# First pairs of a retention and gated feed-forward kernel: the last query multiply behind a mask, its transposes into another bank, and two groups of matmuls issued earlier

## The chip, the cores and the metric

The program runs on one core of a Trainium2 chip. The core has TensorE (PE in the profile; PEld is its weight load), VectorE (DVE), ScalarE (ACT), GpSimd (POOL) and SyncE (SP), which issues the DMAs here. Each engine works through its own queue in order; engines wait for each other by semaphores. The metric is the device time of one execution in microseconds (us).

## The reference

The inputs q, k, v are 8 batches x 8 heads x 576 positions x 64 numbers, all float32. A retention layer feeds a gated feed-forward layer:

```
scores = q @ k^T / sqrt(64)
ret    = (scores * gamma[h] ** (i - j) for j <= i, else 0) @ v      # gamma[h] = 1 - 2 ** (-5 - h)
x      = ret, heads side by side                                    # 4608 x 512
out    = (sigmoid(x @ w_gate) * (x @ w_val)) @ w_out                # d_ff = 1536, out 4608 x 512
```

## The kernel before

**The mathematics.** The decay splits into a factor of the row and one of the column, so q is multiplied by a table (`qtab`, with 1/sqrt(64) in it) and k by another (`ktab`), and the scores need only a triangular mask. Positions are cut into chunks. Within a chunk, the masked scores are multiplied with v (`intra`); what comes from earlier chunks is a 64x64 state per head, the sum of k^T v so far, multiplied with q (`inter`). Both go into the same accumulator, and their sum is a block of `xT`, the transposed input of the feed-forward part.

**The beginning.** The first rows are handled in pairs of chunks: `PAIRS` names pair 0 and pair 1 (256 rows each, both of batch 0) and pair 2 (batch 1, much later). In a pair, chunk `a` lies on partitions `64a` to `64a+63`, with two rows `r` in each partition; the four head pairs `m` are treated in two halves `g`. For one pair and half:

- `cast_pair("k" or "q" or "v", A, g, ...)` turns a loaded tile into bfloat16; for k (GpSimd, L272) and q (VectorE, L272) it is the multiply with the table, for v a cast (GpSimd, L269).
- `turn("k" or "q", A, g, bank)` makes four transposes on TensorE (L312, into `kTp` or `qTp`) and one copy on ScalarE (L322).
- `pair_qk(A, g, banks)` makes 16 score matmuls (L331, `qkp`) into two banks and two masks on VectorE (L336, `ptp`).
- `first_st(A, a)` adds chunk a's k^T v to the running state in the accumulator `st_0` (8 matmuls, L362, `st`); `tile_sv(A, a)` copies the state out by two ScalarE copies (L371, `sbd`). The next `first_st` has to wait for that copy, since it adds to the same accumulator.
- `pair_intra(A, g, a)` is 8 matmuls (L429, `pvp`), `pair_inter(A, a)` 4 (L439, they read `sbd`), `pair_out(A, a, ...)` the copy into `xT` (L448).

`fill(n)` issues n matmuls of zeros, 512 columns each, into a bank that nobody reads (`idle`, L183); `idle_bank()` takes such a bank out of the pool.

**Banks.** The accumulators come from pools. `TR` is one bank (the k transposes, then chunk 1's `pvp`), `PV` is one (the q transposes, then chunk 0's `pvp`), `QK` two, `FF` (the pool `ffn_psum`) three, handed out in turn: the fourth request gets the first bank, when its last reader is done. `turn("q", 1, 1)` without a bank takes from `FF`.

**The order is written by hand** (`manual_schedule`): each engine gets its instructions in the order of the calls. After the pairs, the feed-forward of the first 512 columns begins, in halves of 256 columns (`h_half`: four matmuls each, L895; `gate` on ScalarE, L901; the product on VectorE, L898) for the first two of twelve feature blocks, then in full width (`h_both`, L816). From then on feed-forward matmuls (L712, L779) and the attention of the remaining chunks alternate.

**Loads.** All loads are issued by SP in the order k, q of the first two pairs, v, then the weights `wg`, `wv` for the first features, the second features and so on. Weights are cast to bfloat16 by GpSimd mostly (`cast_w`, L246); the first `h_half("v", ...)` needs both casts of `wv_sb` for features 0 and 1.

Of the kernel before, what the change touches and what calls it, by code (L numbers as in the profile page):

```python
# [16 lines left out]
def kernel(  # L17
# [88 lines left out]
    def half(x):  # L106
        return slice(x * 64, x * 64 + 64)
# [66 lines left out]
    def idle_bank():  # L174
        idle.append(ffn_psum.tile([P, 4, P], FP32, tag="ffn", name=f"idle_{len(idle)}"))
# [3 lines left out]
    def fill(n, parts=1):  # L179

        for i in range(n * parts):
            k = 4 // parts
            nc.tensor.matmul(idle[-1][:, 0:k, :], lhsT=blank, rhs=blank.unsqueeze(1).to_broadcast([P, k, P]),  # L183
                             start=True, stop=True)
# [74 lines left out]
    def cast_pair(nm, A, g, eng):  # L259

        if (nm, A) not in natural:
            natural[nm, A] = osb_pool.tile([P, 2, H, D], BF16, tag="osb", name=f"{nm}p_{A}")
        if nm != "v" and A == 2:
            o = natural[nm, A].rearrange("p r (m y) d -> p y m r d", y=2)[:, g]
        else:
            o = natural[nm, A][:, :, g * M:(g + 1) * M, :].rearrange("p r h d -> p h r d")
        i = parts.pop((nm, "pair", A, g))
        if nm == "v":
            eng(out=o, in_=i)  # L269
        else:  # L270
            tab = (ktab2 if nm == "k" else qtab2)[:, PAIRS[A][1], g * M:(g + 1) * M, :].unsqueeze(3).to_broadcast([P, M, 2, D])
            eng.tensor_tensor(out=o, in0=i, in1=tab, op=ALU.mult)  # L272
# [34 lines left out]
    def pair_t(nm, A, g, psum, tag, eng):  # L307
        ps = psum.tile([P, 2, 2, P], BF16, tag=tag, name=f"{nm}Tp_{A}_{g}")
        for i in range(2):
            for r in range(2):  # L310
                m = 2 * g + i
                nc.tensor.matmul(ps[:, i, r, :], lhsT=natural[nm, A][:, r, 2 * m:2 * m + 2, :], rhs=ident,  # L312
                                 is_transpose=True, start=(i == 0 and r == 0), stop=(i == 1 and r == 1))
        if nm == "k":
            if g == 0:
                turned["kp", A] = osb_pool.tile([P, M, 2, P], BF16, tag="osb", name=f"kT_{A}")
            o = turned["kp", A][:, 2 * g:2 * g + 2]
        else:
            if g == 0:
                turned["qp", A] = osb_pool.tile([P, M, 2 * P], BF16, tag="osb", name=f"qT_{A}")  # L320
            o = turned["qp", A][:, 2 * g:2 * g + 2, :].rearrange("p m (t r) -> p m r t", r=2)
        eng(out=o, in_=ps)  # L322

    def pair_qk(A, g, banks):
        ps = [psum.tile([P, 2, 2, P], FP32, tag=tag, name=f"qkp_{A}_{g}_{hh}") for hh, (psum, tag) in enumerate(banks)]
        for i in range(2):
            m = 2 * g + i
            for r in range(2):
                for a in range(2):
                    for hh in range(2):  # L330
                        nc.tensor.matmul(ps[hh][half(a), i, r, :], lhsT=turned["kp", A][half(hh), m, r, half(a)],  # L331
                                         rhs=turned["qp", A][half(hh), m, a * P:(a + 1) * P], start=True, stop=True)
        if g == 0:
            probs["p", A] = [att_pool.tile([P, M, 2, P], BF16, tag="T", name=f"ptp_{A}_{hh}", bufs=6) for hh in range(2)]
        for hh in range(2):
            nc.vector.tensor_tensor(out=probs["p", A][hh][:, 2 * g:2 * g + 2], in0=ps[hh],  # L336
                                    in1=trip.unsqueeze(1).to_broadcast([P, 2, 2, P]), op=ALU.mult)
# [18 lines left out]
    def first_st(A, a):  # L356

        if 0 not in st_tiles:
            st_tiles[0] = st_psum.tile([P, M, P], FP32, tag="st", name="st_0")
        for r in range(2):  # L360
            for m in range(M):
                nc.tensor.matmul(st_tiles[0][:, m, :], lhsT=natural["k", A][half(a), r, 2 * m:2 * m + 2, :],  # L362
                                 rhs=natural["v", A][half(a), r, 2 * m:2 * m + 2, :],
                                 start=(A == 0 and a == 0 and r == 0 and m == 0),
                                 stop=(A == 1 and a == 1 and r == 1 and m == M - 1), skip_group_check=True)

    def tile_sv(A, a, engs):
        b, a2 = PAIRS[A]
        sb = sbd[2 * A + a]
        for hh in range(2):  # L370
            engs[hh](out=sb[half(hh), :, half(hh)], in_=st_tiles[b][half(hh), :, half(hh)])  # L371
        state[b, 2 * a2 + a, 1] = sb
# [3 lines left out]
    def pair_tile(A, a, banks):  # L376

        s = 2 * A + a
        ps = [psum.tile([P, M // len(banks), P], FP32, tag=tag, name=f"pvp_{s}_{i}") for i, (psum, tag) in enumerate(banks)]
        pair_ps[s] = [(ps[m * len(banks) // M], m % (M // len(banks)), M // len(banks)) for m in range(M)]  # L380
# [39 lines left out]
    def pair_intra(A, g, a):  # L420
        s = 2 * A + a
        if s not in pair_ps:
            pair_tile(A, a, [(tr_psum, "tr") if a else (pv_psum, "pv")])
        for i in range(2):
            m = 2 * g + i
            ps, at_m, of = pair_ps[s][m]
            for r in range(2):
                for hh in range(2):
                    nc.tensor.matmul(ps[half(hh), at_m, :], lhsT=natural["v", A][half(a), r, 2 * m + hh, :],  # L429
                                     rhs=probs["p", A][hh][half(a), m, r, :],  # L430
                                     start=(at_m == 0 and r == 0), stop=(at_m == of - 1 and r == 1),
                                     skip_group_check=True)

    def pair_inter(A, a):
        b, a2 = PAIRS[A]
        c = 2 * a2 + a
        for m in range(M):
            ps, at_m, of = pair_ps[2 * A + a][m]
            nc.tensor.matmul(ps[:, at_m, :], lhsT=state[b, c - 1, 1][:, m, :],  # L439
                             rhs=turned["qp", A][:, m, a * P:(a + 1) * P],  # L440
                             start=False, stop=(at_m == of - 1), skip_group_check=True)

    def pair_out(A, a, *engs):
        t0 = (2 * A + a) * P
        k = M // len(engs)
        for i, eng in enumerate(engs):
            ps, at_m, _ = pair_ps[2 * A + a][i * k]
            eng(out=xT[:, i * k:(i + 1) * k, t0:t0 + P], in_=ps[:, at_m:at_m + k])  # L448
# [356 lines left out]
    def turn(nm, A, g, pool=ffn_psum, tag="ffn"):  # L805
        pair_t(nm, A, g, pool, tag, on_act)
# [34 lines left out]
    FF = [(ffn_psum, "ffn"), (ffn_psum, "ffn")]  # L841
    TR, PV = (tr_psum, "tr"), (pv_psum, "pv")
# [8 lines left out]
    turn("q", 0, 1, *PV)  # L851
    fill(3)
    cast_pair("q", 1, 0, nc.vector)
    cast_pair("q", 1, 1, nc.vector)
    pair_qk(0, 1, FF)
    turn("k", 1, 0, *TR)
    turn("q", 1, 0, *PV)
    fill(2)
    turn("k", 1, 1, *TR)
    turn("q", 1, 1)  # L860
    idle_bank()
    fill(1)
    pair_qk(1, 0, QK)
    fill(1)
    first_st(0, 0)
    tile_sv(0, 0, (on_act, on_act))
    pair_intra(0, 0, 0)
    pair_intra(0, 0, 1)
    pair_intra(0, 1, 0)
    pair_qk(1, 1, FF)  # L870
    pair_out(0, 0, on_act)
    pair_intra(0, 1, 1)
    first_st(0, 1)
    pair_inter(0, 1)
    tile_sv(0, 1, (on_act, on_act))
    pair_out(0, 1, on_dve)
    for a in range(2):
# [13 lines left out]
    def h_half(what, fc, x, ps):  # L891

        cols = slice(x * 256, x * 256 + 256)
        for kc in range(NKC):
            nc.tensor.matmul(ps, lhsT=(wg_sb if what == "g" else wv_sb)[:, kc, fc * P:(fc + 1) * P], rhs=xT[:, kc, cols],  # L895
                             start=(kc == 0), stop=(kc == NKC - 1))
        if what == "v":
            nc.vector.tensor_tensor(out=gvs[fc][:, cols], in0=gs[fc][:, cols], in1=ps, op=ALU.mult)  # L898

    def gate(fc, x, ps):  # L900
        nc.scalar.activation(out=gs[fc][:, x * 256:x * 256 + 256], in_=ps, func=AF.Sigmoid)  # L901

    def h_bank(psum, tag, name, n):
        return psum.tile([P, n, 256], FP32, tag=tag, name=name)
# [6 lines left out]
    pair_inter(1, 1)  # L911
    pair_out(1, 1, on_dve, on_act)
    gate(1, 0, g1)
    v0 = h_bank(ffn_psum, "ffn", "hv_0", 2)
    h_half("v", 0, 0, v0[:, 0])
    h_half("g", 0, 1, (g2 := h_bank(qk_psum, "qk", "hg_2", 2))[:, 0])
# [1 line left out]
    h_half("v", 1, 0, v0[:, 1])  # L918
    gate(0, 1, g2[:, 0])
    gate(1, 1, g2[:, 1])  # L920
    first_st(1, 1)
    tile_sv(1, 1, (on_act, on_act))
    for fc in range(2):
        h_half("v", fc, 1, h_bank(ffn_psum, "ffn", f"hv_{1 + fc}", 1)[:, 0])
# [162 lines left out]
```

## Time and profile before

| what | value |
|---|---|
| median of 4 runs | 329.68 us (329.45 to 330.28) |
| the profiled execution | 330.28 us, of which the span of the instructions is 328.6 us |
| PE busy | 318.1 us, 97% of the span |
| DVE, ACT, POOL busy | 149.1, 140.0, 104.8 us |
| chain that ended last | PE 91%, SP issue 3%, DMA 2%, DVE 1%, issue 1% |
| granted TensorE clock | 1.00 in every stretch of the stage table |
| DMA | q1: 54.44 MB, 68.9% of 16 engines' span; close to 100% of them busy until about 140 us |

Times in the profile count from the start of the span. A row of the timeline gives start, duration, engine, line, operation, the tiles (written `<-` read), how many instructions are merged, and in brackets how long the engine had been idle and what ended the wait. Matmuls overlap: a matmul's result comes about 0.16 us after the next one may begin, so the pace is read from one start to the next, not from durations. A row of the chain is start, duration and what the chain passed through.

The stretch that the change touches is the first 23 us. Up to about 12 us, the engines follow the loads as they land; from 22.8 us on, TensorE runs almost without a gap to the end.

### The profile page before, as it was taken

How to read it: one execution, taken by the hardware profiler on the slowest of the kernel's cores; microseconds unless marked ns; L12 is line 12 of the kernel's file. 1: busy time of each engine (PE TensorE's matmuls, PEld its weight loads, DVE VectorE, ACT ScalarE, POOL GpSimd, SP SyncE). 2: the span in 40 equal slices, each digit the busy share in tenths (PEclk: the TensorE clock that was granted, in tenths of full speed). 3: DMA queues.
4: the chain of work that ended last, by engine and by line, in shares of the span. 5: the costliest groups of instructions: out<-in, count | busy, mean ns of one | idle time of the engine just before them, and what ended most of it. 6: DMA issues, size and time to landing. Idle time of an engine off the chain costs nothing.

```text
span 328.6 us, 8723 instructions
## 1 busy us (share of the span) xinstructions
PE 318.1 (97%) x3586; PEld 170.5 (52%) x3620; DVE 149.1 (45%) x334; ACT 140.0 (43%) x315; POOL 104.8 (32%) x138
## 2 busy tenths in 40 slices
PE   7899999999999999999999999999999999999995
PEld 6564456856646654455444544454445544544443
DVE  5854747756615463345344543334444434404410
ACT  5645454554424444325533453335334533343321
POOL 5765647454534554008300840065003000000000
PEclk9999999999999999999999999999999999999999
DMA  7999999999997999908890799259804810010003
GB/s 215 309 358 381 340 295 230 220 188 201 185 208 156 220 231 217 170 0 190 203 229 22 141 205 254 47 112 224 212 0 101 324 61 0 34 69 31 3 32 96
DMA packets 144793, 55.14 MB, mean 168 GB/s; under 512 B 125168, under 2 KB 136688, under 8 KB 144752
## 3 DMA queue, kind: packets, MB, share of 16 engines
q1 hardware_dynamic: 144608, 54.44, 68.9%
q8 instruction: 28, 0.46, 0.6%
q10 hardware_dynamic: 144, 0.13, 0.1%
q14 instruction: 13, 0.11, 0.1%
HBM read 37.75 MB, written 9.44 MB: 144 GB/s over the span
## 4 chain that ended last, share of the span: by engine, by line
PE 91%; SPq 3%; DMA 2%; issue 1%; DVE 1%; ACT 0%; POOL 0%; ACTq 0%
PE h L712 50%; PE op L779 24%; PE op L966 3%; SPq L130 3%; PE hv L816 3%; PE hg L816 3%; DMA wv<-in_moe_w_val_dram 2%; PE val L523 2%; PE row L497 1%; PE row L505 1%; PE val L539 1%; PE op L768 1%; PE hv L895 1%; SPq L142 0%; PE hg L895 0%
## 5 line engine op out<-in xcount | busy, mean ns | idle before, releaser
L740 DVE TENSOR_TENSOR gv<-g,h 128x512 bf16<-128x512 bf16 (+1 forms) x96 | 62.8, 654 | 103.2 <-PE h L712 100.5
L712 PE MATMUL h<-xT,wv_sb 128*128 128x512 bf16 (+2 forms) x426 | 100.4, 356 | 0.3
L712 PE MATMUL h<-xT,wg_sb 128*128 128x512 bf16 (+2 forms) x426 | 100.4, 355 | 0.3
L736 ACT ACTIVATE g<-h 128x512 bf16<-128x512 f32 (+1 forms) x96 | 54.7, 570 | 94.3 <-PE h L712 90.1
L779 PE MATMUL op<-wo_sb,gv 128*128 128x512 bf16 x355 | 80.7, 379 | 2.2 <-issue 2.1
L712 PEld LDWEIGHTS <-wg_sb 128*128 128x128 bf16 x432 | 42.0, 98 | 41.2
L712 PEld LDWEIGHTS <-wv_sb 128*128 128x128 bf16 x432 | 41.9, 98 | 40.4
L779 PEld LDWEIGHTS <-gv 128*128 128x128 bf16 x372 | 35.3, 98 | 40.9
L290 POOL CAST v<-v 128x512 bf16<-128x512 f32 x29 | 17.7, 609 | 89.3 <-PE val L523 80.5
L285 POOL TENSOR_TENSOR qk<-k,ktab 128x512 bf16<-128x512 f32 x30 | 31.3, 1042 | 32.5 <-DMA k<-in_k_dram 18.7
L755 ACT COPY ob<-op 128x512 f32<-128x512 f32 x33 | 19.3, 585 | 35.9 <-PE op L779 33.0
L285 POOL TENSOR_TENSOR qk<-q,qtab 128x512 bf16<-128x512 f32 x28 | 29.6, 1058 | 1.5 <-DMA q<-in_q_dram 1.5
L512 DVE TENSOR_TENSOR pt<-row,tri 128x256 bf16<-128x256 f32 x60 | 21.6, 418 | 14.0 <-PE row L505 12.5
L581 ACT CAST xT<-val 128x256 bf16<-128x256 f32 x46 | 15.0, 380 | 22.6 <-PE val L539 18.0
L624 DVE TENSOR_TENSOR s<-s,row 128x256 f32<-128x256 f32 x39 | 16.3, 417 | 1.3
L473 ACT CAST sb<-s 128x256 bf16<-128x256 f32 x44 | 15.9, 421 | 0.3 <-DVE s L624 0.2
L567 DVE COPY glance<-val 128x1 f32<-128x1 f32 x24 | 2.7, 155 | 23.3 <-PE val L539 22.6
L966 PE MATMUL op<-wo_sb,gv 128*128 128x512 bf16 x45 | 11.4, 380 | 0.3 <-issue 0.2
L523 PEld LDWEIGHTS <-v 64*64 64x64 bf16 x480 | 6.2, 108 | 7.5 <-issue 7.5
L539 PE MATMUL val<-T,sb 64*64 64x64 bf16 x368 | 9.7, 195 | 0.3 <-DVE glance L567 0.3
L823 DVE TENSOR_TENSOR gv<-g,hv 128x512 bf16<-128x512 bf16 x10 | 6.8, 685 | 6.8 <-PE hv L816 6.8
L497 PE MATMUL row<-T 64*64 64x64 bf16 x480 | 9.7, 196 | 0.0
(104 smaller groups left out, 239.2 us busy)
## 6 DMA issues: line engine op xcount, KB each, us to landing
out_dram<-ob SPq DMA_DIRECT2D x31, 256.0 KB, 3.0
k<-in_k_dram SPq DMA_DIRECT2D x26, 256.0 KB, 3.9
q<-in_q_dram SPq DMA_DIRECT2D x26, 256.0 KB, 4.4
v<-in_v_dram SPq DMA_DIRECT2D x26, 256.0 KB, 4.7
wg<-in_moe_w_gate_dram SPq DMA_DIRECT2D x12, 256.0 KB, 5.2
wv<-in_moe_w_val_dram SPq DMA_DIRECT2D x12, 256.0 KB, 5.2
wo<-in_moe_w_out_dram SPq DMA_DIRECT2D x12, 256.0 KB, 5.1
k32p<-in_k_dram SPq DMA_DIRECT2D x6, 256.0 KB, 5.4
```

Of the source, the lines that this page charges most:

```text
L285: eng.tensor_tensor(out=natural_qk[s][:, i].rearrange("p m (y d) -> p y m d", y=2), in0=by_halves(loaded[s][1 - i]), in1=tab, op=ALU.mult)
L290: eng(out=natural["v", s], in_=loaded[s][2])
L473: eng(out=state[key], in_=src)
L512: nc.vector.tensor_tensor(out=probs[s][:, y], in0=row_ps[s][y][:, 0], in1=tri.unsqueeze(1).to_broadcast([P, M, 64]), op=ALU.mult)
L624: nc.vector.tensor_tensor(out=new, in0=running[b], in1=p, op=ALU.add)
L712: nc.tensor.matmul(out, lhsT=w_sb[:, kc, fc * P:(fc + 1) * P], rhs=xT[:, kc, t0 + a:t0 + e], start=(kc == 0), stop=(kc == NKC - 1))
L736: nc.scalar.activation(out=g[:, 0:n], in_=h1[:, 0:n], func=AF.Sigmoid)
L740: nc.vector.tensor_tensor(out=gvs[some[0]][:, a:e], in0=g[:, 0:n], in1=h2[:, 0:n], op=ALU.mult)
L755: (eng or on_act)(out=ob, in_=opp)
L779: nc.tensor.matmul(opp, lhsT=gvs[fc][:, nb * P:(nb + 1) * P], rhs=wo_sb[:, fc, :], start=(fc == 0), stop=(fc == NFC - 1))
L816: nc.tensor.matmul(ps, lhsT=(wg_sb if what == "g" else wv_sb)[:, kc, fc * P:(fc + 1) * P], rhs=xT[:, kc, 0:4 * P], start=(kc == 0), stop=( ...
L966: nc.tensor.matmul(opps[nb], lhsT=gvs[fc][:, nb * P:(nb + 1) * P], rhs=wo_sb[:, fc, :], start=(fc == 0), stop=(fc == NFC - 1))
```

## The change

Five edits, all in the order of calls:

1. The masks of pair 0's second half (`pair_qk(0, 1, FF)`) are put in front of the last query multiply (`cast_pair("q", 1, 1)`) on VectorE.
2. `turn("q", 1, 1)` goes into the bank `TR` instead of one of `FF`, and is issued behind the third scores (`pair_qk(1, 0, QK)`), no longer in front of them.
3. One `idle_bank()` and two `fill(1)` are left out.
4. The value matmuls of pair 0 (`pair_intra`) are grouped by chunk: both halves of the heads for chunk 0, then the scores `pair_qk(1, 1)`, then both halves for chunk 1; and `pair_inter(0, 1)` goes in front of `first_st(0, 1)`.
5. `first_st(1, 1)`, the last state product of the two pairs, is issued right behind `pair_out(1, 1)` and `gate(1, 0)`, in front of the four `h_half` groups that it followed. Its copies `tile_sv(1, 1)` stay where they were.

```diff
     cast_pair("q", 1, 0, nc.vector)
+    pair_qk(0, 1, FF)
     cast_pair("q", 1, 1, nc.vector)
-    pair_qk(0, 1, FF)
     turn("k", 1, 0, *TR)
     turn("q", 1, 0, *PV)
     fill(2)
     turn("k", 1, 1, *TR)
-    turn("q", 1, 1)
-    idle_bank()
-    fill(1)
     pair_qk(1, 0, QK)
-    fill(1)
+    turn("q", 1, 1, *TR)
     first_st(0, 0)
     tile_sv(0, 0, (on_act, on_act))
-    pair_intra(0, 0, 0)
-    pair_intra(0, 0, 1)
-    pair_intra(0, 1, 0)
+    for g in range(2):
+        pair_intra(0, g, 0)
     pair_qk(1, 1, FF)
     pair_out(0, 0, on_act)
-    pair_intra(0, 1, 1)
+    for g in range(2):
+        pair_intra(0, g, 1)
+    pair_inter(0, 1)
     first_st(0, 1)
-    pair_inter(0, 1)
     tile_sv(0, 1, (on_act, on_act))
...
     gate(1, 0, g1)
+    first_st(1, 1)
     v0 = h_bank(ffn_psum, "ffn", "hv_0", 2)
     h_half("v", 0, 0, v0[:, 0])
...
     gate(1, 1, g2[:, 1])
-    first_st(1, 1)
     tile_sv(1, 1, (on_act, on_act))
```

## The prediction

> **What bounds the kernel now.** I read the chain of waits first, then TensorE's own waits, then the timelines of single engines between 10 and 23 us. From 23 us on the chain is matmul after matmul, and all waits of TensorE after 19 us come to under 3 us, most of them its own issue. So a microsecond saved before 23 us stays saved, if no load is late afterwards; nothing else in the change can matter. The chain runs through this load:
>
> ```profile
> 12.03 6.84 DMA wv<-in_moe_w_val_dram
> 18.86 0.05 issue
> 18.92 0.62 POOL wv_sb L246
> ```
>
> TensorE's timeline shows the last wait of the beginning and the work behind it:
>
> ```profile
> 18.81 0.40 PE L439 MATMUL pvp<-qT,sbd 128*128 128x128 bf16 x4
> 19.05 0.38 PE L895 MATMUL hv<-xT,wv_sb 128*128 128x256 bf16 x2
> 19.59 0.39 PE L895 MATMUL hv<-xT,wv_sb 128*128 128x256 bf16 x2 [0.16 <-POOL wv_sb L246]
> 19.81 1.13 PE L895 MATMUL hg<-xT,wg_sb 128*128 128x256 bf16 x8
> 20.78 0.60 PE L895 MATMUL hv<-xT,wv_sb 128*128 128x256 bf16 x4
> 21.31 0.62 PE L362 MATMUL st<-vp,kp 64*128 64x128 bf16 x8
> 21.86 1.05 PE L895 MATMUL hv<-xT,wv_sb 128*128 128x256 bf16 x8
> 22.75 0.38 PE L816 MATMUL hg<-xT,wg_sb 128*128 128x512 bf16 x1
> ```
>
> The weights `wv_sb` come late: GpSimd waits 1.84 us for their load and casts until 19.53. The state products `st` stand behind this wait, where every matmul counts. What leads up to it, on VectorE, TensorE and ScalarE:
>
> ```profile
> 9.88 0.68 DVE L272 TENSOR_TENSOR qp<-q32p,qtab 128x512 bf16<-128x512 f32 x1
> 10.91 1.10 DVE L272 TENSOR_TENSOR qp<-q32p,qtab 128x512 bf16<-128x512 f32 x1 [0.35 <-DMA q32p<-in_q_dram]
> 11.93 1.27 DVE L336 TENSOR_TENSOR ptp<-qkp,trip 128x512 bf16<-128x512 f32 x2
> ```
> ```profile
> 12.66 0.38 PE L312 MATMUL qTp<-ident,qp 128*128 128x128 bf16 x4 [0.71 <-DVE ptp L336]
> 12.88 0.38 PE L183 MATMUL idle<-blank 128*128 128x512 bf16 x1
> ...
> 13.54 0.39 PE L183 MATMUL idle<-blank 128*128 128x512 bf16 x1
> 13.87 0.62 PE L362 MATMUL st<-vp,kp 64*128 64x128 bf16 x8
> ```
> ```profile
> 13.09 0.74 ACT L322 COPY qT<-qTp 128x512 bf16<-128x512 bf16 x1 [0.48 <-PE qTp L312]
> 14.52 0.74 ACT L371 CAST sbd<-st 64x256 bf16<-64x256 f32 x2 [0.70 <-PE st L362]
> 15.29 0.58 ACT L448 CAST xT<-pvp 128x512 bf16<-128x512 f32 x1
> 15.95 0.74 ACT L371 CAST sbd<-st 64x256 bf16<-64x256 f32 x2
> 18.01 0.74 ACT L371 CAST sbd<-st 64x256 bf16<-64x256 f32 x2 [1.31 <-PE st L362]
> ```
>
> To be seen: the last transposes wait 0.71 us though their q was ready at 12.01; the wait ends with a mask, which frees their bank of `FF`. And the states form a chain: products, ScalarE copy, `pair_inter`, next products.
>
> **The move of the last state products.** They cost what separates 20.78 from 21.86 beyond the four `hv` matmuls: eight `hv` take 22.75 - 21.86 = 0.89, four 0.44, so 1.08 - 0.44 = 0.64 us, the changes between full and half array included. Gone there, this is 0.64 us saved. In the new place they cost the same 0.64 us, between `pair_inter(1, 1)` and the first `hv`, where today TensorE idles 0.16 us. To be hidden, TensorE has to come there earlier by 0.64 - 0.16, about 0.5 us; the other edits must bring this. ScalarE's copies of this state stay in place and wait for nothing new.
>
> **The last query multiply: its end E.** The scores of L331 end at 10.57 and masks follow scores by 0.05 us, so the masks now run from 10.60. A successor starts 1.20 after a pair of masks (8.69 to 9.88 in the same timeline): the multiply starts at 11.80, its load having landed at 10.89. Alone it takes 0.68 (row of 9.88). It took 1.10 when GpSimd's multiply was already running for 0.55 us of it; now GpSimd's first cast of v starts at 11.73 and takes 0.61, so I add 0.34 and get E = 12.82, against 12.01 before. Bounds: 12.48 (0.68) and 12.91 (1.10). Behind it on VectorE wait only the masks of the third scores, which end by 14.1 and are wanted by pair 1's value matmuls after 15.5. The load that takes this q's buffer is the 26th, issued after 19.6 us: nothing lost on SP's queue. GpSimd's and SP's orders are untouched.
>
> **The new bank.** `TR` is free when ScalarE has copied k's turn (12.00 + 0.60 = 12.60), before E: no price. The scores ahead of it wait for ScalarE's copy until 12.16 and take 0.20: no price either. Chunk 1's `pvp` now waits in `TR` for the copy of q's turn, E + 1.26, and is wanted only after the scores that need the same copy.
>
> **Fills.** Two of 0.21 us leave TensorE before the first state products. They lie on its path there, but the chain below is set by ScalarE, so I count nothing for them by themselves.
>
> **The chain from E to the weights.** Transposes at E + 0.10; copy from E + 0.52 to E + 1.26 (rows 12.66, 13.09). First state products from E + 0.43, done E + 1.05; ScalarE copies the state right behind the copy of q, to E + 2.0. That is 14.82 against 15.26 now. Meanwhile TensorE has 16 value matmuls, 16 scores and 16 value matmuls, from E + 0.98. In the trace, four row and column quarters run at once, and matmuls of two calls overlap; all 48 take 0.76. Grouped by chunk, a value group uses one row half: 16 in 0.44, so 0.66 if the halves of neighbouring groups still overlap, 1.10 if not. With a change of array shape (0.15), `pair_inter(0, 1)` starts between E + 2.03 and E + 2.23. Its four take 0.18, another change 0.15; the second state products start at E + 2.36 to 2.56, are done 0.62 later, and copied (0.03 + 0.74) at E + 3.75 to 3.95. `pair_inter(1, 0)` follows at E + 3.79 to 3.99, i.e. 16.61 to 16.81, against 17.03. TensorE's own work is done before (about E + 3.55), the masks too. From there to `pair_inter(1, 1)` nothing changes: 18.81 - 17.03 = 1.78, so 18.39 to 18.59. Then 0.33, the last products 0.40, a change 0.15: the first `hv` at 19.27 to 19.47, two of them 0.22, and the pair that needs the late weights could start at 19.49 to 19.69. The weights allow 19.59. The middle of mine is the same: the products are just hidden.
>
> The Trainium skill, TensorEngine Tiling (Array Packing), Key Properties, speaks against edit 4: tiles work in parallel, and a change of tiling mode drains the array. The grouping by chunk gives up half of the tiles and adds no fewer changes. By the page alone I would take 1.10 for the 48 matmuls and end about 0.1 us late, for a gain of 0.63. The row shows scores starting between value matmuls of another call, so the lost half is partly filled; I keep the middle.
>
> **Sum.** 0.64 for the products; 0.09 because the third `hg` no longer waits (eight `hg` take 0.97 now against 0.89 of the eight `hv`; its ScalarE copy into `xT` comes 0.3 us earlier); minus 0.03 for the half of cases in which my chain ends after 19.59. Gain 0.70 us. In the profiled execution that is 330.28 - 0.70 = 329.58 (span 327.9, with the same 1.7 around it). That execution was 0.60 above the median of the runs; the same step from the median gives 328.98, say 329.0. With E and the 48 matmuls at their late bounds the chain ends 0.16 late: gain about 0.57. If the weights land earlier, and E is 12.48, up to 1.1.
>
> **What is late next.** Weights are fixed by their landing, and TensorE comes 0.7 us sooner. The tightest: the last `wg` cast for features 4 to 7 ends at 25.17 and is used at 26.63, 1.46 later; v of pair 2 is cast at 43.00 and used at 44.70. Both keep over 0.7 us. The transposed chunk wanted at 64.8 landed at 60.1. So the gain should last.
>
> **Rivals.**
> - *The chain is longer than I add it up* (no change). Some fifteen hops are added by rows with errors of a few hundredths each; if they come to 0.5 us, or the multiply is held longer by GpSimd, the products are back on the path. Against it: the first copies move by 0.4 us by plain order. For it: nothing after E has slack over 0.1. It would give 329.3 to 329.7.
> - *More than the weights allow.* If the runs have the load earlier than the profiled 18.86 (1.8 us of GpSimd waiting for one load, while its neighbours follow at 0.65), the chain alone counts: 0.9 to 1.1, so 328.6 to 328.8.
> - *TensorE's clock drops* (slower). Two fills go, and new idle stretches of 0.3 to 0.5 us come at 11.8, 12.4 and 16.4. The first 40 fills took 4.35 us, 0.109 each against 0.055 for the same width at 12.7: half speed costs 0.055 per 128 columns. If it fell for matmul work of more than 0.7 us in a stretch that TensorE bounds, the gain is gone; over 2 us of work it gives 331. Against: the granted clock is 1.00 around today's gaps of 0.81 and 0.71. No run here shows how idle it must be. The Trainium skill, TensorE: Matmul & The Clock Gate, PE-mode transpose, says transposes do not count as busy for the gate; fills would, which speaks against the edit.
>
> **How the numbers follow.** 0.2% is 0.66 us, about what a measurement of this kernel tells from no change; my 0.70 lies just beyond it. Hidden as worked out: 0.60 (328.7 to 329.2), of which two thirds beyond the bound; more: 0.10; longer chain, no change: 0.16; slower: 0.14. Together faster 0.50, same 0.36, slower 0.14. Range 328.55 to 329.8: it leaves out the slower cases and the end of the early-weights one.
>
> **What would show it.** `qTp` of pair 1 near 12.9 in `TR`, no wait for a mask; VectorE's last multiply at 11.8, 0.7 to 1.1 long; `pair_inter(1, 0)` before 16.9; `st` at 18.7 to 18.9 in front of `hv`; the first full-width `hg` near 22.0. Wrong if `hv` begins after 19.7, if the clock is below 1, or if a wait for weights appears at 25 to 45 us.

## The result

The changed kernel takes 329.09 us (median of 34 runs), the kernel before 329.74 us (median of 55). The ratio is 0.9981, with a 95% interval of 0.9976 to 0.9986: 0.65 us faster, 0.46 to 0.8 us by the interval. The profiled execution took 328.88 us with a span of 327.1.

TensorE's last wait of the beginning is gone, and the last state products (`st`) stand in front of `hv`. TensorE's timeline of the changed kernel, from the last `pair_inter` on:

```profile
17.61 0.40 PE L439 MATMUL pvp<-qT,sbd 128*128 128x128 bf16 x4
17.94 0.62 PE L362 MATMUL st<-vp,kp 64*128 64x128 bf16 x8
18.49 0.61 PE L892 MATMUL hv<-xT,wv_sb 128*128 128x256 bf16 x4
18.94 1.04 PE L892 MATMUL hg<-xT,wg_sb 128*128 128x256 bf16 x8
19.81 1.47 PE L892 MATMUL hv<-xT,wv_sb 128*128 128x256 bf16 x12
21.12 1.89 PE L816 MATMUL hg<-xT,wg_sb 128*128 128x512 bf16 x7
```

The four `hv` run without a gap: there is no wait for weights in this execution. GpSimd's two casts of `wv_sb` follow each other from 16.28 and end at 17.56:

```profile
16.28 1.27 POOL L246 CAST wv_sb<-wv 128x512 bf16<-128x512 f32 x2
```

The first full-width `hg` starts at 21.12 instead of 22.75, which is 1.63 us, more than the change is worth. The loads of this execution landed up to 2 us sooner than in the first profile of before. So the two traces have to be compared from a point that the change doesn't touch: the start of pair 0's second scores, called S from here on (the row of L331 at 10.15 in the kernel before, 9.28 in the changed one). From S to the first full-width `hg` it is 12.60 us before and 11.84 after: **0.76 us saved**. From that `hg` to the end it is 305.81 and 306.01 us, and between 305.8 and 306.3 in all thirteen profiles of this study: nothing behind it waits for what the change moved. What edits 1 to 4 made of the way to it, on VectorE, ScalarE and TensorE of the changed kernel:

```profile
9.74 1.29 DVE L336 TENSOR_TENSOR ptp<-qkp,trip 128x512 bf16<-128x512 f32 x2 [0.25 <-PE qkp L331]
10.94 1.03 DVE L272 TENSOR_TENSOR qp<-q32p,qtab 128x512 bf16<-128x512 f32 x1
```
```profile
12.47 0.73 ACT L322 COPY qT<-qTp 128x512 bf16<-128x512 bf16 x1 [0.73 <-PE qTp L312]
13.06 0.74 ACT L371 CAST sbd<-st 64x256 bf16<-64x256 f32 x2
...
15.03 0.74 ACT L371 CAST sbd<-st 64x256 bf16<-64x256 f32 x2 [0.61 <-PE st L362]
```
```profile
12.03 0.40 PE L312 MATMUL qTp<-ident,qp 128*128 128x128 bf16 x4 [0.28 <-DVE qp L272]
...
14.05 0.40 PE L439 MATMUL pvp<-qT,sbd 128*128 128x128 bf16 x4
14.38 0.62 PE L362 MATMUL st<-vp,kp 64*128 64x128 bf16 x8
...
15.83 0.40 PE L439 MATMUL pvp<-qT,sbd 128*128 128x128 bf16 x4 [0.22 <-ACT sbd L371]
```

The multiply ends at 11.97, and the transposes follow it without waiting for a mask. TensorE then waits once, for ScalarE's copy of the second state (`sbd`).

All runs by S, in us. E is the end of the last query multiply; the first `hv`, the third `hg` (the one that needs ScalarE's copy into `xT`) and the full width are starts, the weights cast is the end of GpSimd's second cast of `wv_sb`; times against before are medians with the interval of the ratio where there is one.

| kernel | E | first `hv` | weights cast | third `hg` | full width | time | ratio to before |
|---|---|---|---|---|---|---|---|
| before, first profile | 1.86 | 8.90 | 9.38 | 9.98 | 12.60 | 329.74 | |
| before_again | 1.87 | 8.90 | 7.99 | 9.99 | 12.60 | | |
| changed | 2.70 | 9.21 | 8.28 | 9.88 | 11.84 | 329.09 | 0.9981 [0.9976, 0.9986] |
| products_alone | 1.70 | 9.39 | 7.85 | 10.05 | 12.02 | 329.14 | 0.9979 [0.9971, 0.9988] |
| chain_alone | 2.40 | 8.31 | 8.22 | 9.40 | 12.02 | 329.45 | 0.9994 [0.9982, 1.0006] |
| fills_back | 2.35 | 9.10 | 7.80 | 9.76 | 11.73 | 329.01 | 0.9972 [0.9962, 0.9983] |
| grouping_undone | 2.75 | 9.11 | 8.62 | 9.78 | 11.74 | 329.04 | 0.9975 [0.9966, 0.9984] |
| lag_before_multiply | 2.69 | 9.21 | 8.15 | 9.88 | 11.84 | 329.05 | 0.9984 [0.9974, 0.9993] |
| lag_twice | 2.96 | 9.48 | 8.63 | 10.14 | 12.11 | 329.54 | 0.9992 [0.9983, 1.0001] |
| late_weights_before | 1.68 | 8.72 | 9.72 | 10.22 | 12.85 | | |
| late_weights_changed | 2.70 | 9.23 | 10.43 | 10.93 | 12.89 | | |
| old_order_free_bank | 2.70 | 8.93 | 7.74 | 9.59 | 11.56 | 328.77 | 0.9973 [0.9963, 0.9984] |
| multiply_between_masks | 1.87 | 8.70 | 7.70 | 9.36 | 11.32 | 328.52 | 0.9969 [0.9958, 0.9979] |

A ratio's interval is some 0.3 us wide on either side for the experiments, so for effects of 0.1 to 0.4 us the profiles counted from S carry the verdict, and the times only have to agree.

### The profile page after: what moved, and what is told of

Same layout as the page of the kernel before. It is cut to its first block, busy times and chain, and to the rows that moved or that the text cites. A ratio compares the mean times of both kernels' runs of the same rounds, so it can differ in the third digit from the quotient of the medians.

```text
span 327.1 us, 8719 instructions
## 1 busy us (share of the span) xinstructions
PE 317.7 (97%) x3584; PEld 171.0 (52%) x3618; DVE 148.3 (45%) x334; ACT 139.5 (43%) x315; POOL 104.9 (32%) x138
## 4 chain that ended last, share of the span: by engine, by line
PE 95%; issue 1%; DVE 1%; ACT 1%; ACTq 0%
PE h L712 50%; PE op L779 24%; PE op L963 3%; PE hv L816 3%; PE hg L816 3%; PE val L523 2%; PE idle L183 1%; PE row L497 1%; PE row L505 1%; PE val L539 1%; PE op L768 1%; PE st L362 1%; PE hg L892 1%; PE hv L892 1%; PE qkp L331 1%
```

## The experiments

### What covers the products

My theory on record was that the products hide behind the wait for the late weights, once the other edits bring TensorE there 0.5 us earlier. The first question was whether this wait is there at all, so the kernel before was profiled once more, without any edit.

> The kernel before, once more, for a second profile. Theory W: if the second load of the first wv lands about 9.9 us after pair 0's second q load, as in the changed kernel's profile (11.0 in the first profile of before), then hv runs without a wait for weights and the third hg waits about 0.42 us for ScalarE's copy into xT; the first full-width hg comes 14.88 us after that q load, as in the first profile. If the weights were what bound it, it would come earlier by up to 0.3 us.

TensorE's timeline of the kernel before in this second profile:

```profile
18.20 0.40 PE L439 MATMUL pvp<-qT,sbd 128*128 128x128 bf16 x4
18.44 0.60 PE L895 MATMUL hv<-xT,wv_sb 128*128 128x256 bf16 x4
19.12 1.22 PE L895 MATMUL hg<-xT,wg_sb 128*128 128x256 bf16 x8
20.17 0.60 PE L895 MATMUL hv<-xT,wv_sb 128*128 128x256 bf16 x4
20.71 0.62 PE L362 MATMUL st<-vp,kp 64*128 64x128 bf16 x8
21.26 1.05 PE L895 MATMUL hv<-xT,wv_sb 128*128 128x256 bf16 x8
22.14 1.03 PE L816 MATMUL hg<-xT,wg_sb 128*128 128x512 bf16 x3
```

The weights were ready at 17.52, and `hv` ran at once. But the four `hv` are through at 18.88, and `hg` starts at 19.12: it waits 0.24 us for VectorE's copy into `xT`, and its third matmul, at 19.53, another 0.19 for ScalarE's. These are the two copies:

```profile
18.64 0.42 DVE L448 CAST xT<-pvp 128x256 bf16<-128x256 f32 x1 [1.09 <-PE pvp L439]
19.10 0.37 ACT L448 CAST xT<-pvp 128x256 bf16<-128x256 f32 x1 [0.54 <-DVE xT L448]
```

The full width still starts 12.60 us after S. So the kernel before has two waits in this place: one for the weights, if they are late, which lets the third `hg` start 9.89 after S, and one for `xT`, in both profiles, which ends at 9.98. The first hid most of the second from me. In the eleven profiles that keep the order of loads, the weights were late once, in the one that I predicted from.

The two halves of the change, each alone. Edit 5:

```diff
     gate(1, 0, g1)
+    first_st(1, 1)
...
     gate(1, 1, g2[:, 1])
-    first_st(1, 1)
     tile_sv(1, 1, (on_act, on_act))
```

> The kernel before with edit 5 alone: the last state products right behind gate(1, 0), all else as before. Theory W (there is a wait behind pair_inter(1, 1) in which the products hide: for the late weights, or, if these are early, for ScalarE's copy into xT that the third hg needs): TensorE has about 0.42 us there between the end of its work and 20.13 in the profile of before, the products take 0.64, so 0.22 is paid there and 0.64 saved later: 0.42 us faster than before, 329.3. Theory N (nothing covers them; the gain of the whole change is the earlier chain): 0.0 to 0.1 faster, 329.65 to 329.75. Theory E (edit 5 needs the other edits, as the sum on record says: 0.5 us earlier first): 0.1 to 0.25 faster.

TensorE's timeline (S is 9.76):

```profile
18.27 0.40 PE L439 MATMUL pvp<-qT,sbd 128*128 128x128 bf16 x4
18.60 0.62 PE L362 MATMUL st<-vp,kp 64*128 64x128 bf16 x8
19.15 0.61 PE L895 MATMUL hv<-xT,wv_sb 128*128 128x256 bf16 x4
19.60 1.04 PE L895 MATMUL hg<-xT,wg_sb 128*128 128x256 bf16 x8
20.47 1.47 PE L895 MATMUL hv<-xT,wv_sb 128*128 128x256 bf16 x12
21.78 1.89 PE L816 MATMUL hg<-xT,wg_sb 128*128 128x512 bf16 x7
```

329.14 us, and 12.02 us from S to full width, 0.58 less than before. Of this, 0.16 is not the edit's: E came 0.16 sooner after S in this execution (1.70 against 1.86), since the load of that q landed sooner. That leaves 0.42 us, as theory W had it: TensorE has 0.42 us of waiting behind `pair_inter(1, 1)`, the products fill it and 0.22 us more, and 0.64 is saved later. Edit 5 doesn't need the other edits, against what I had on record. The measured time, 0.65 us below before with an interval of 0.4 to 1.0, has 0.42 just inside it. By the times alone the split would not be known (329.14 here, 329.09 with all edits); it rests on one profile of each kernel.

Edits 1 to 4 without edit 5:

```diff
     gate(1, 0, g1)
-    first_st(1, 1)
...
     gate(1, 1, g2[:, 1])
+    first_st(1, 1)
     tile_sv(1, 1, (on_act, on_act))
```

> The changed kernel without edit 5: the last state products back behind the four halves of the feed-forward. Theory W: the chain comes 0.3 us earlier; with early weights this is the gain, 0.3 us, 329.4; with late weights only 0.09, 329.65. Theory N: the whole gain of 0.65, 329.1. The two halves should add up to the whole under W with early weights (0.42 + 0.31 against the measured 0.65).

329.45 us, not told apart from before by its times. In the profile 12.02, but with E at 2.40: the multiply took 0.74 here and 1.03 in the changed kernel, and the transposes behind it began 2.51 after S instead of 2.75. With these 0.24 us (that they carry through one for one is shown by lag_twice below) it would be 12.26, 0.34 less than before; I had 0.3. So 0.42 and 0.34 make the 0.76 of the whole: the halves add up, and theory N, that nothing covers the products, is out.

Then the case that the prediction assumed, weights late in any case: the second load of the first `wv` is issued behind three loads of the next features, in the changed kernel and in the one before. `load_w` gets a third argument for this, the loads that it issues (its own lines are left out here).

```diff
-    load_w(0, 2)
-    load_w(2, 2)
+    load_w(0, 2, (("g", 0), ("g", 1), ("v", 0)))
+    load_w(2, 2, (("g", 0), ("g", 1), ("v", 0)))
+    load_w(0, 2, (("v", 1),))
+    load_w(2, 2, (("v", 1),))
```

> The changed kernel with the second load of the first wv issued behind three loads of the next features, about 2 us later. TensorE then has to wait for these weights in any case, and the state products of edit 5 lie wholly in front of the wait: hv's third matmul about 0.9 us later than without, the first full-width hg at about 15.0 us after pair 0's second q load instead of 14.14. Compared with the kernel before with the same loads (to be run), 0.64 us earlier: the products' own cost.

> The kernel before with the second load of the first wv issued behind three loads of the next features, as in the run of the changed kernel with that order. There, hv's third matmul followed the cast by 0.05 us and the first full-width hg followed the cast by 2.46 us. Here the products stand behind the wait: first full-width hg 2.46 + 0.64 = 3.10 us after the cast. So in a case where the weights bind, edit 5 alone is worth 0.64 and the other edits nothing. If the products had another cover behind the weights, the distance would be under 3.0.

TensorE's timelines, first of the changed kernel, then of the one before, both with late weights:

```profile
18.39 0.39 PE L896 MATMUL hv<-xT,wv_sb 128*128 128x256 bf16 x2
19.65 0.39 PE L896 MATMUL hv<-xT,wv_sb 128*128 128x256 bf16 x2 [0.86 <-POOL wv_sb L250]
...
22.06 1.24 PE L820 MATMUL hg<-xT,wg_sb 128*128 128x512 bf16 x4
```
```profile
19.24 0.39 PE L899 MATMUL hv<-xT,wv_sb 128*128 128x256 bf16 x2 [0.68 <-POOL wv_sb L250]
...
20.88 0.62 PE L366 MATMUL st<-vp,kp 64*128 64x128 bf16 x8
...
22.31 1.03 PE L820 MATMUL hg<-xT,wg_sb 128*128 128x512 bf16 x3
```

From the third `hv` to full width it is 22.06 - 19.65 = 2.41 us with the products in front and 22.31 - 19.24 = 3.07 behind: 0.66 us. That is the products' price (0.64 on record), and in this case the other edits give nothing. From cast to full width it is 2.46 and 3.13 us, with 3.10 expected. Only the lateness itself was a little more than I had: 1.04 us for the third `hv` instead of 0.9, 15.18 us from the q load instead of 15.0.

### What sets the changed kernel's start of `hv`

A memset of 256 columns in front of the last query multiply, to make E late:

```diff
     pair_qk(0, 1, FF)
+    lag = consts.tile([P, 2 * P], FP32, name="lag")
+    nc.vector.memset(lag, 0.0)
     cast_pair("q", 1, 1, nc.vector)
```

> The changed kernel with a memset of 256 float32 columns on VectorE (0.27 us in the kernel before for the same width) between the masks and the last query multiply, so that E comes 0.27 us later. Theory C (in the changed kernel the chain from E through the state copies sets the start of hv, 6.5 us after E, and the weights wait for it): the first full-width hg comes 0.27 us later, counted from the landing of pair 0's second q load (14.41 us instead of 14.14), the kernel 0.2 to 0.3 us slower than the changed one, 329.35. Theory L (the late weights set it, as I had it on record): 0.0 to 0.1 slower. GpSimd may now be busy in another part of the multiply, which moves its own time between 0.68 and 1.10.

The full width came 11.84 after S, the same as without. That looked like theory L. But E hadn't moved either, 2.69. VectorE's timeline:

```profile
11.41 0.27 DVE L856 MEMSET lag<- 128x256 f32 x1
11.60 0.75 DVE L272 TENSOR_TENSOR qp<-q32p,qtab 128x512 bf16<-128x512 f32 x1
```

The multiply began later and took 0.75 instead of 1.03. GpSimd's first cast of v ends 2.15 us after S in both kernels, and the multiply ends 0.54 to 0.55 us after that cast in both. So this run tells nothing of C and L. With a second memset:

> The changed kernel with two memsets of 0.27 us between the masks and the last query multiply. With one, the multiply began after GpSimd's cast instead of during it and took 0.75 instead of 1.03, so E did not move. With two it has to: E 0.2 to 0.6 us later, counted from the start of pair 0's second scores (2.70 in the changed kernel). Theory C (the chain from E sets hv): the first full-width hg later by the same amount (11.84 in the changed kernel), 0.2 to 0.5 us slower than the changed one. Theory L (weights set it): no later than 0.1.

```profile
12.34 0.63 DVE L272 TENSOR_TENSOR qp<-q32p,qtab 128x512 bf16<-128x512 f32 x1
```

Now E is 2.96, 0.26 later, and the full width 12.11, 0.27 later. The time is 329.54, 0.45 above the changed kernel. Theory C holds: in the changed kernel the chain from E sets `hv`, one for one; the weights were cast 0.85 us before the first `hv` here, and 0.93 in the changed kernel's profile.

### The single edits

The two fills of edit 3 back, around the third scores:

```diff
     turn("k", 1, 1, *TR)
+    fill(1)
     pair_qk(1, 0, QK)
+    fill(1)
     turn("q", 1, 1, *TR)
```

> The changed kernel with the two fills of edit 3 back, one on each side of the third scores. If they only fill idle time (TensorE idles 0.25 us before the third scores and 0.28 before the last transposes in the changed kernel's profile): the time of the changed kernel within 0.05 us, 329.1. If what counts is that TensorE has 0.43 us less to do before the first state products: 0.43 slower than the changed kernel, 329.5. If the clock mattered: a granted clock below 1 in the changed kernel and not here; both show 1.0.

329.01 us: no loss. The profile is not quite the test that I wanted, since E came early (2.35), and there the second fill held the transposes until 2.64, 0.24 longer than E asked; with E at 2.70 it fits into the idle time. The granted clock is 1.0 here and 0.999 in the changed kernel's profile, and matmuls keep their pace (the twelve `hv` in front of the full width take 1.31 us in both): taking the fills out did nothing to the clock.

Edit 4 undone:

```diff
-    for g in range(2):
-        pair_intra(0, g, 0)
+    pair_intra(0, 0, 0)
+    pair_intra(0, 0, 1)
+    pair_intra(0, 1, 0)
     pair_qk(1, 1, FF)
     pair_out(0, 0, on_act)
-    for g in range(2):
-        pair_intra(0, g, 1)
-    pair_inter(0, 1)
+    pair_intra(0, 1, 1)
     first_st(0, 1)
+    pair_inter(0, 1)
```

> The changed kernel with edit 4 undone: value matmuls of pair 0 in the old order and the second state products in front of pair_inter(0, 1). Theory S (the state copies on ScalarE set the pace, and edit 4 puts 0.33 us of pair_inter in front of the second products): pair_inter(1, 0) 0.2 to 0.35 us earlier after E than in the changed kernel (E + 3.85 there), so 0.2 to 0.35 us faster than it, 328.8, as far as the weights allow. Rival (the old order makes chunk 1's first values wait in TR for the copy of q's turn, and the grouping avoids this): 0.1 to 0.3 slower than the changed kernel, 329.2 to 329.4.

11.74 with E 0.05 later than in the changed kernel: 0.10 earlier as it stands, 0.15 for the same E. So edit 4 costs a little; it is not what makes the change faster. It gave less than my 0.2 to 0.35, because chunk 1's first values now wait in `TR` for the copy of q's turn (from 13.65 to 13.74): the rival's mechanism, with the smaller price of the two.

Both together: the old order, and the last q turn in a bank of `FF`, which is free now that the masks come first.

```diff
-    turn("q", 1, 1, *TR)
+    turn("q", 1, 1)
```

and the edits of the run above.

> Edits 1, 3 and 5 and the later place of the last q turn kept; the turn in a bank of FF again, edit 4 undone. With the masks in front, a bank of FF is free when the turn comes, and TR is free for chunk 1's values, so value matmuls of both row halves run side by side. Theory S (pace set by E, state copies and TensorE's work between them): second state products at about E + 1.9 instead of E + 2.40, pair_inter(1, 0) at about E + 3.5 instead of E + 3.85: 0.35 us faster than the changed kernel, 328.75. Rival (bank of FF still held by a mask, or TensorE's work is the limit): no more than the 0.15 that undoing edit 4 alone gave in the profiles, 328.95.

TensorE's timeline, to be held against 14.05 to 15.83 of the changed kernel above (S is 9.49 here, 0.21 later):

```profile
14.07 0.60 PE L362 MATMUL st<-vp,kp 64*128 64x128 bf16 x8
14.61 0.40 PE L439 MATMUL pvp<-qT,sbd 128*128 128x128 bf16 x4
14.94 0.89 PE L429 MATMUL pvp<-ptp,vp 64*64 64x128 bf16 x32
15.76 0.40 PE L439 MATMUL pvp<-qT,sbd 128*128 128x128 bf16 x4
```

The second state products start 4.58 after S instead of 5.10, `pair_inter(1, 0)` has no wait left, and the full width comes at 11.56: 0.28 us less than the changed kernel. With that wait gone, TensorE's own work is what is left in this stretch, and I had expected 0.35.

Last, against this version, the multiply between the two masks, and its turn in front of the third scores (`pair_qk` gets one more argument, which it calls behind the first mask; its own lines are left out):

```diff
-    pair_qk(0, 1, FF)
-    cast_pair("q", 1, 1, nc.vector)
+    pair_qk(0, 1, FF, lambda: cast_pair("q", 1, 1, nc.vector))
...
-    pair_qk(1, 0, QK)
-    turn("q", 1, 1)
+    turn("q", 1, 1)
+    pair_qk(1, 0, QK)
```

> The version with the old order and a free bank, and the last query multiply between the two masks of pair 0's second half instead of behind both; its turn in front of the third scores. The multiply then begins about 1.05 us after these scores start, before GpSimd's first cast of v (1.54 after), and takes 0.68: E at 1.75 instead of 2.70. If E sets the pace to the end: the first full-width hg up to 0.9 us earlier (10.7 instead of 11.56). My estimate: the casts of v then hold the first state products (third matmul after GpSimd's second cast, about 2.9), so 0.3 us: 11.25, and 328.5 us. If TensorE's own work sets it from there: no gain, 328.77.

VectorE's and TensorE's timelines:

```profile
10.02 0.69 DVE L336 TENSOR_TENSOR ptp<-qkp,trip 128x512 bf16<-128x512 f32 x1
10.63 0.80 DVE L272 TENSOR_TENSOR qp<-q32p,qtab 128x512 bf16<-128x512 f32 x1
11.36 0.68 DVE L336 TENSOR_TENSOR ptp<-qkp,trip 128x512 bf16<-128x512 f32 x1
```
```profile
12.16 0.89 PE L364 MATMUL st<-vp,kp 64*128 64x128 bf16 x8
```

E is 1.87, 0.83 earlier, and the first state products stretch to 0.89 instead of 0.63: the third of them starts at 12.56, behind GpSimd's second cast of v, which ends at 12.51. The full width comes at 11.32, the time is 328.52 us: 0.57 us below the changed kernel's median, and the fastest of the study. Its ratio to before is 0.9969.

## Why the prediction was right, and where not

The time, 329.09 against 329.0, and the gain, 0.65 against 0.70, came out, and most steps did too.

- **The products' price.** 0.64 on record; 0.66 between the two runs with late weights. Right.
- **E.** On record 2.67 after S (12.82 - 10.15); measured 2.70, with the multiply at 1.03 against the 1.02 I took. Right, with some luck: I took 1.02 for 0.54 us of GpSimd's work beside the multiply (11.80 to 12.34), but for 0.54 the runs show 1.09 (grouping_undone); here it was 0.49. The bounds of 0.68 and 1.10 are what the other runs show (0.63 to 1.09).
- **The chain from E.** On record `pair_inter(0, 1)` at E + 2.03 to 2.23, `pair_inter(1, 0)` at E + 3.79 to 3.99, `hv` at E + 6.45 to 6.65; measured 2.07, 3.85 and 6.51. Right. That this chain, and not the weights, sets `hv` was shown by lag_twice; that it can be shortened behind E, by old_order_free_bank.
- **The 48 matmuls.** On record 0.66 to 1.10 for the grouped order; 0.98 measured (12.92 to 14.05, less 0.15 for the change of shape) against 0.76 before. The lost row half is only partly filled: the truth lies halfway between the middle that I kept (0.88) and the 1.10 without any overlap. Edit 4 as a whole cost 0.1 to 0.15 us, as grouping_undone shows.
- **The bank and the fills.** Both at no price against the kernel before; right, but `FF` would have been free as well, and `TR` costs 0.1 to 0.15 once the old order is taken.
- **The cover.** This is the step that failed: "the products are just hidden" by the wait for the weights, and they need the other edits to get there. In ten of eleven profiles there is no such wait. The products fill the wait for the copies into `xT`, which I had listed as a separate 0.09, and they give 0.42 without any other edit. I also misread the idle time: 0.16 counts from the end of the matmul before, but by starts the next could have begun at 19.05 + 0.22 = 19.27 and began at 19.59, so 0.32, and with the 0.09 behind it some 0.4 us were there to be filled, not 0.16. That the sum came out all the same is luck: both waits end within 0.1 us of each other, 9.89 and 9.98 after S, and what I called 0.64 plus 0.09 minus 0.03 is 0.42 from the products and 0.34 from the earlier chain.
- **The rival of early weights** (0.9 to 1.1) was sized wrong for the same reason. The weights were early in the changed kernel's profile, and the gain counted from S was 0.76: E at 2.70, not the 2.33 that this rival needs, decides then. With the E on record, the chain itself let the third `hv` start at 19.49 to 19.69 and the weights at 19.59, so that early weights alone could add 0.1 at most.
- **The slower rival** (clock) did not come: the granted clock is 0.998 to 1.0 in all profiles. That alone would not show it, since the granted clock is 1.00 too in the first 5.3 us of before, where the 40 fills start 0.107 us apart. What shows it is the pace: the twelve `hv` of the changed kernel start 0.109 us apart, the eight of before 0.111.
- **Late afterwards.** Nothing was: 305.8 to 306.3 us from the first full-width matmul on, in all kernels, whether it came at 20.9 or 22.8.
- **A sum.** With both late bounds the chain on record ends 0.18 late, not 0.16 (0.10 from the 48 matmuls, 0.08 from E, whose bound is 11.80 + 1.10 = 12.90). Nothing hung on it.

The profiles say 0.76, the medians 0.65 with an interval of 0.46 to 0.8. Both agree. Where in the interval the true gain lies is not shown: landings move S by up to 1 us between executions.

## What to carry to other kernels

A wait that ends last may hide a second one that ends just before it; before an edit is costed by the wait that it fills, look what would have ended the idle time if the first releaser had been early, and profile the kernel before a second time if that releaser is a load. Compare two traces from a point upstream of the edit that both share, not from the start of the span: loads moved that point by up to 1 us here, more than the change was worth. In a hand-written order, an instruction that only has to be early for one consumer (a multiply) can go between two that are needed late (masks): that gave another 0.24 us here.

## What the runs showed of the hardware

VectorE's multiply of q, with both operands in SBUF, took 0.68 or 0.69 us where GpSimd had nothing under way when it began (0.63 once, in lag_twice). Where a GpSimd instruction had begun before it and ran on for at least 0.16 us beside it, the multiply ended 0.54 to 0.55 us after that instruction, in all 33 such cases of the thirteen profiles, and took 0.71 to 1.10 us. The other way round, a cast of v that began during the last multiply ended 0.47 us after it, once in each of the thirteen profiles, and took 0.71 to 1.08 us instead of 0.61. The masks, with one operand in PSUM, took 0.67 to 0.69 in either case. In the changed kernel, GpSimd's casts before and behind the start of the multiply (10.94 to 11.97):

```profile
10.82 0.61 POOL L269 CAST vp<-v32p 128x512 bf16<-128x512 f32 x1 [0.43 <-DMA v32p<-in_v_dram]
```
```profile
11.55 0.90 POOL L269 CAST vp<-v32p 128x512 bf16<-128x512 f32 x1
```

The Trainium skill, SBUF — State Buffer, Who interferes with whom, has the rule: a VectorE instruction with two SBUF inputs contends with a GpSimd instruction that reads SBUF, and the order of issue decides who is held. The page calls it an exclusive lock. The rows agree with both: of the instruction that came second, only the first 0.13 or 0.14 us (0.68 - 0.55, 0.61 - 0.47) could lie beside the other.

So in the changed kernel it is the first cast of v that sets E: it ends 2.15 us after S, and E is 2.70. In chain_alone, where that load landed 0.3 us sooner after S, the cast ends at 1.86 and E is 2.40. And 0.27 us of idle work in front of the multiply cost nothing (lag_before_multiply), since the cast still ended at 2.15.

The second load of the first `wv` landed 16.6 to 18.0 us into the span in ten profiles, 0.65 to 0.7 us after the load before it, and at 18.86 in one, 2.45 us after the load before it. What held it there is not shown by any run.
